# Nine period boundaries of a fused mixer move by one step

## The chip, the cores and the metric

The kernel runs on one core of a Trainium2 chip. The metric is the device time of one execution in microseconds; the time before is the median of three runs. A core has a matrix engine (TensorE; PE for its matmuls and PEld for its weight loads in the profile), VectorE (DVE), ScalarE (ACT), GpSimd (POOL) and SyncE (SP), which here issues the DMAs. Each engine runs its own instructions in the order in which the program lists them, and engines wait for each other by semaphores.

## The reference

Two parts follow each other. The first is a linear attention with a decaying state (batch B = 4, 8 heads, 768 tokens, 48 wide per head):

```
for t in range(S):
    cur = einsum('bhd,bhe->bhde', u * kt, vt)
    y[t] = einsum('bhd,bhde->bhe', rt, state + cur)
    state = w * state + einsum('bhd,bhe->bhde', kt, vt)
```

Its output, put together to x of 4 x 768 x 384, goes into a gated mixer:

```
h = relu(x @ w_in);  u, v = h[..., :512], h[..., 512:]
v_n = (v - mean(v)) / sqrt(var(v) + 1e-6)
v_s = einsum('ts,bsd->btd', w_spatial, v_n) + b_spatial
out = (u * v_s) @ w_out
```

## The kernel before, in words

**Attention.** The tokens of a batch are cut into 6 chunks of 128, so there are NM = 24 chunks, numbered through the batches; chunk m belongs to batch m // 6. For each chunk there are five pieces. `load_chunk` issues the two DMAs of a chunk (tiles rk and rkv, 512 and 648 KB). `prep` gives four parts that scale and combine the inputs on DVE and POOL and form the diagonal term (lines 279 to 308). `g1(m)` (lines 312 to 331) makes the scores and the state products with small matmuls into the PSUM tile ps: 32 in line 320 and 32 in line 329, or 16 there for the last chunk of a batch. `mid(m)` (339 to 360) masks the scores into the tile a (line 343, DVE), writes the state into the tiles sblk through `block` (lines 336 and 337, ACT) and updates the state on DVE. `g2(m)` (362 to 389) multiplies these with r and v, all in line 369: 48 matmuls with the state (24 for the first chunk of a batch) and 64 with a. `fin` casts the result to the pair xh and xl, a high and a low part (lines 399 and 404).

**Mixer.** The mixer works in steps, and each product is three matmuls of high and low parts (`mm3`, lines 427 to 430). A `moe_v` step makes the gate half of one chunk (9 matmuls, 512 columns), and after the third and sixth of a batch the normalisation follows on ACT and DVE. A `moe_u` step makes one 128-wide slice of the other half for 384 tokens (9 matmuls), `moe_sp` the spatial product for such a slice (18 matmuls, then an add on DVE, a product on POOL and a split into high and low on ACT and DVE), and `moe_out` the output product for 128 tokens (12 matmuls, a copy on ACT, an output DMA on SP). Every matmul has a weight load of its own. There are 28 steps a batch and 112 in all, in one list `steps` whose order is written out in lines 547 to 560.

**The order of the work.** The loop in lines 605 to 661 runs over periods i, one per chunk. At a period's start stand `g2(i)`, `fin(i)`, `g1(i + 1)` and `mid(i + 1)`, and the load of chunk i + 3. Then follow the mixer's steps from the list, until `done` has reached `n`, the number of steps that shall be done by the end of the period; between them, one ahead of each step, the four parts of the preparation of chunk i + 2. What remains of the parts follows after the last step. A step may hand work to a later step with `later`, which counts steps and not periods. Line 627 sets n: for the first six periods from the list FIRST, for the last all 112, and for the others an even deal:

```
int(10 + (i - 5) * 28 / 6)
```

which gives 14, 19, 24, 28, 33, 38, 42, ... 84, 89 for periods 6 to 22, that is 4 or 5 steps a period, and leaves 23 steps for period 23. TensorE's order is the order of the program: g2, g1, steps, g2, g1, steps.

## Time and profile before

| | before |
|---|---|
| median of 3 runs | 374.99 us (372.95 to 376.47) |
| profiled execution, its own time | 374.84 us |
| its span, first to last instruction | 373.1 us |
| TensorE matmuls busy | 340.5 us, 91% of the span |
| TensorE weight loads busy | 310.8 us, 83% |
| DVE, POOL, ACT busy | 200.5, 157.0, 148.0 us |
| mean granted TensorE clock | 0.993 of full speed |

How to read the rows: a row of the waits names who waited, for whom, the total in us, how often, and the longest. "issue" is time in which an engine waited for nothing that the profile shows. A row of the chain of waits has start, length and what ran. A row of the timeline has start, length, engine, line, operation, output and input, shape, and the number of instructions merged into it; an idle time in front of them stands in brackets. A row of the windows table has the stretch, its length, and for PE, PEld, DVE, ACT and POOL in turn the busy time with the number of instructions in brackets, then the granted clock, the DMA share and the rate in GB/s. Semaphore instructions are not in these counts. A row of the DMA queues has packets, MB and the time of the packets as a share of 16 engines' span. A row of the groups has line, engine, operation, tiles, shape and number, then busy time in all and mean ns of one, and the idle time before them. A row of the DMA issues has tiles, number, KB each and the us to landing.

### The profile page before, as it was taken

To read this page: it belongs to the slowest core of one execution; us is meant where nothing else is said; L and a number is where in the kernel's file an instruction comes from. 1 tells how busy PE (TensorE), PEld (TensorE's weight loads), DVE (VectorE), ACT (ScalarE), POOL (GpSimd) and SP (SyncE) were. 2 spreads that over 40 slices of the span, in tenths; PEclk is the share of its full clock that TensorE was granted. 3 is DMA by queue.
4 is the path that set the end of the run, shared out by engine and by line. 5 is a ranking of instruction groups with operands and counts; after the bars stand their busy time and mean duration, and the time that the engine had idled before them with its cause. 6 is when DMAs were issued, how large, how long until landed. Compare 5 with 4: busy or idle time off the path is not lost.

```text
span 373.1 us, 12304 instructions
## 1 busy us (share of the span) xinstructions
PE 340.5 (91%) x5479; PEld 310.8 (83%) x5479; DVE 200.5 (54%) x400; ACT 148.0 (40%) x325; POOL 157.0 (42%) x160
## 2 busy tenths in 40 slices
PE   2759669879999999899999989998999899999994
PEld 1427558779999998799999978898989898999994
DVE  7697855879645553664362625686451624433130
ACT  3154558584123234546131324645131336461211
POOL 5975555763554261645753444043652320013120
PEclk9999999999999999999999999999999999999998
DMA  7994755433031441333031352134041010000101
GB/s 251 413 372 135 267 204 176 170 129 105 29 124 70 131 154 52 117 132 129 2 129 65 129 186 67 72 129 131 0 152 45 2 66 4 0 0 2 56 9 63
DMA packets 14021, 41.69 MB, mean 112 GB/s; under 512 B 1680, under 2 KB 6416, under 8 KB 13968
## 3 DMA queue, kind: packets, MB, share of 16 engines
q1 hardware_dynamic: 13968, 40.90, 31.2%
q8 instruction: 43, 0.70, 0.8%
q14 instruction: 10, 0.08, 0.1%
HBM read 36.18 MB, written 4.72 MB: 110 GB/s over the span
## 4 chain that ended last, share of the span: by engine, by line
PE 82%; DVE 5%; ACT 4%; issue 4%; DMA 2%; POOL 2%; SPq 0%; ACTq 0%; DVEq 0%
PE pm L428 21%; PE pm L429 20%; PE pm L430 20%; PE xp L369 10%; PE ps L320 3%; PE ps L329 3%; DMA rkv<-rkvN 2%; ACT vs L472 1%; DVE a L343 1%; ACT ws_h L182 1%; DVE ws_l L183 1%; PE pm L498 1%; PE pm L503 1%; PE pm L499 1%; PE pm L226 1%
## 5 line engine op out<-in xcount | busy, mean ns | idle before, releaser
L516 POOL TENSOR_TENSOR g<-g,u 128x384 f32<-128x384 f32 x31 | 31.5, 1015 | 116.8 <-DVE g L515 116.7
L428 PE MATMUL pm<-ws_h,vnorm 128*128 128x384 f32 x192 | 64.9, 338 | 0.0
L430 PE MATMUL pm<-ws_h,vnorm 128*128 128x384 f32 x192 | 64.3, 335 | 0.0
L429 PE MATMUL pm<-ws_l,vnorm 128*128 128x384 f32 x192 | 64.2, 334 | 0.0
L303 POOL TENSOR_TENSOR a<-diag,dg 128x512 f32<-128x512 f32 x24 | 25.4, 1059 | 66.8 <-DVE dg L294 33.7
L182 ACT CAST gt<-g 128x384 fp32r<-128x384 f32 x32 | 16.4, 514 | 91.3 <-POOL g L516 89.3
L183 DVE TENSOR_TENSOR gt<-g,gt 128x384 fp32r<-128x384 f32 x32 | 20.9, 654 | 57.0 <-ACT gt L182 57.0
L428 PEld LDWEIGHTS pm<-ws_h,vnorm 128*128 128x128 f32 x192 | 36.0, 188 | 0.3
L429 PEld LDWEIGHTS pm<-ws_l,vnorm 128*128 128x128 f32 x192 | 36.0, 188 | 0.0
L430 PEld LDWEIGHTS pm<-ws_h,vnorm 128*128 128x128 f32 x192 | 36.0, 188 | 0.0
L428 PE MATMUL pm<-wo_h,gt 128*128 128x384 f32 x96 | 32.9, 343 | 0.0
L430 PE MATMUL pm<-wo_h,gt 128*128 128x384 f32 x96 | 32.3, 336 | 0.0
L429 PE MATMUL pm<-wo_l,gt 128*128 128x384 f32 x96 | 32.3, 336 | 0.0
L515 DVE TENSOR_TENSOR g<-pm,bb 128x384 f32<-128x384 f32 x32 | 17.7, 553 | 22.1 <-PE pm L430 22.0
L329 PE MATMUL ps<-rkv 64*64 64x48 f32 x704 | 17.8, 221 | 12.3 <-issue 8.7
L428 PE MATMUL pm<-wi_h,xh 128*128 128x512 f32 x72 | 28.7, 398 | 0.0
L430 PE MATMUL pm<-wi_h,xl 128*128 128x512 f32 x72 | 28.3, 393 | 0.1
L429 PE MATMUL pm<-wi_l,xh 128*128 128x512 f32 x72 | 28.3, 393 | 0.0
L369 PE MATMUL xp<-a,rkv 64*32 64x64 f32 x1536 | 24.1, 227 | 3.2 <-issue 3.2
L288 POOL TENSOR_TENSOR rkv<-rkv,ub 128x384 f32<-128x384 f32 x24 | 26.1, 1086 | 1.9
L449 DVE BATCH_NORM_STATS2 q<-vs 128x6 f32<-128x512 f32 x24 | 16.5, 687 | 18.6 <-ACT vs L442 18.6
L329 PEld LDWEIGHTS ps<-rkv 64*64 64x64 f32 x704 | 15.1, 139 | 13.5 <-issue 9.7
(112 smaller groups left out, 736.0 us busy)
## 6 DMA issues: line engine op xcount, KB each, us to landing
rkv<-rkvN SPq DMA_DIRECT2D x24, 648.0 KB, 5.8
rk<-rkT SPq DMA_DIRECT2D x24, 512.0 KB, 3.8
out<-ob SPq DMA_DIRECT2D x24, 192.0 KB, 1.9
raw<-w_in SPq DMA_DIRECT2D x6, 512.0 KB, 10.0
wst<-w_sp SPq DMA_DIRECT2D x12, 192.0 KB, 5.7
raw<-w_out SPq DMA_DIRECT2D x4, 384.0 KB, 8.1
bb<-b_sp SPq DMA_DIRECT2D x1, 384.0 KB, 5.6
ub<-uB SPq DMA_DIRECT2D x1, 192.0 KB, 6.6
```

Source lines behind the costliest of these rows:

```text
L182: nc.scalar.copy(hi, src)
L183: (eng or nc.vector).tensor_tensor(out=lo, in0=src, in1=hi.bitcast(F32), op=ALU.subtract)
L288: nc.gpsimd.tensor_tensor(out=rn, in0=rn, in1=ub, op=ALU.mult)
L303: nc.gpsimd.tensor_tensor(out=a.rearrange("s j p t -> s (j p) t"), in0=diag.unsqueeze(1).to_broadcast([P, H, HC]), in1=dg.rearrange("s j p ...
L329: nc.tensor.matmul(ps[64 * j:64 * j + 64, s0 // 64, 256 + p * D:256 + (p + 1) * D], t["kn"][s0:s0 + 64, h * D:h * D + 64], t["v"][s0:s0 + ...
L369: nc.tensor.matmul(xp[32 * g:32 * g + 32, z, jt * HC:(jt + 1) * HC], lhsT, rhs, start=(z, g) not in began, stop=True, skip_group_check=Tru ...
L428: nc.tensor.matmul(o, lh, rh, start=first, stop=False)
L429: nc.tensor.matmul(o, lh, rl, start=False, stop=False)
L430: nc.tensor.matmul(o, ll, rh, start=False, stop=last)
L449: nc.vector.bn_stats(out=q6[:, c % 3, :], in_=vs)
L515: nc.vector.tensor_tensor(out=g, in0=pm[:, 0:TH], in1=bb[:, ts_], op=ALU.add)
L516: (nc.vector if (b, t, d) == (B - 1, 1, ND - 1) else nc.gpsimd).tensor_tensor(out=g, in0=g, in1=u, op=ALU.mult)
```

## The change: nine numbers of done steps

A list of 24 numbers is added to the even deal of line 627. It is zero except in nine periods: the steps done by the end of periods 9, 13, 18 and 21 are one fewer, and by the end of periods 10, 15, 16, 19 and 20 one more. The order of the steps is the same, and so is everything that a step does; what differs is on which side of the next period's g2 and g1 nine of the steps stand.

| after period | done before | done after | step that changes sides |
|---|---|---|---|
| 9 | 28 | 27 | a moe_out of batch 0 goes behind |
| 10 | 33 | 34 | a moe_v of batch 1 comes ahead |
| 13 | 47 | 46 | a moe_sp of batch 1 goes behind |
| 15 | 56 | 57 | a moe_out of batch 1 comes ahead |
| 16 | 61 | 62 | a moe_v of batch 2 comes ahead |
| 18 | 70 | 69 | a moe_u of batch 2 goes behind |
| 19 | 75 | 76 | a moe_out of batch 2 comes ahead |
| 20 | 80 | 81 | a moe_sp of batch 2 comes ahead |
| 21 | 84 | 83 | a moe_out of batch 2 goes behind |

Periods 9 to 22 had 4, 5, 5, 4, 5, 5, 4, 5, 5, 4, 5, 5, 4 and 5 steps, and have 3, 7, 4, 4, 4, 6, 5, 5, 4, 3, 7, 5, 2 and 6.

```diff
+    ADJ = [0, 0, 0, 0, 0, 0, 0, 0, 0, -1, 1, 0, 0, -1, 0, 1, 1, 0, -1, 1, 1, -1, 0, 0]
...
-        n = 0 if i < 0 else FIRST[i] if i < NC else len(steps) if i == NM - 1 else int(10 + (i - 5) * 28 / 6)
+        n = 0 if i < 0 else FIRST[i] if i < NC else len(steps) if i == NM - 1 else int(10 + (i - 5) * 28 / 6) + ADJ[i]
```

## The prediction

> **What bounds the kernel now.** I read the page first, then the waits of TensorE alone, then the chain of waits, then the timeline around one stall, and last a table of windows that counts weight loads.

> ```profile
> span 373.1 us, 12304 instructions
> PE 340.5 (91%) x5479; PEld 310.8 (83%) x5479; DVE 200.5 (54%) x400; ACT 148.0 (40%) x325; POOL 157.0 (42%) x160
> q8 instruction: 43, 0.70, 0.8%
> PE ps L329 <- issue: 4.6, 5, 1.1
> ```

> The last line is the whole answer of the waits for TensorE from 88 us to the end. The first differing step falls in period 9, after 122 us, and the 23 steps of the last period are the same ones in the same order. So in the stretch that can change, the matrix engine waits for no other engine: it is idle 4.6 us in five places, always in line 329, on "issue". Removing all of it would be worth 4.6 us, 1.2% of the run; a reordering can win no more, since every step still costs the same TensorE time. It can lose more, by making PE wait for others.

> The five places in the chain of waits (start, length):

> ```profile
> 149.36 0.96 issue
> 218.50 0.95 issue
> 253.49 1.05 issue
> 273.35 0.62 issue
> 289.85 1.01 issue
> ```

> One of them in TensorE's timeline:

> ```profile
> 250.63 0.88 PE L369 MATMUL xp<-rk,sb 128*32 128x64 f32 x48
> 251.44 0.97 PE L369 MATMUL xp<-a,rkv 64*32 64x64 f32 x64
> 252.34 0.69 PE L320 MATMUL ps<-rk 64*64 64x64 f32 x32
> 252.85 0.63 PE L329 MATMUL ps<-rkv 64*64 64x48 f32 x30
> 254.54 0.31 PE L329 MATMUL ps<-rkv 64*64 64x48 f32 x2 [1.05 <-issue]
> ```

> I call lines 369, 320 and 329 between two periods' steps a burst, numbered by its g2: this is burst 19, 48+64+32+32 = 176 small matmuls with a weight load each (160 in bursts 10, 16 and 22, whose g1 is short, and 152 in 12 and 18, whose g2 is), and it stops before the last two. What is it waiting for? Counting loads answers. The windows below are (first row) burst 6 up to its stall, then bursts 11, 16, 19, 20 and 21 up to theirs, then one stall to the next, then from the stall of burst 11 to the starts of bursts 13 and 14, then the whole of burst 22, and last 6 us of steps. The count behind PEld is what to read.

> ```profile
> 76.85:79.90 3.05, 2.59 (x151) 2.22 (x151) 1.22 (x3) 2.99 (x7) 2.56 (x2) 1.00 0.37 115
> 146.72:149.90 3.18, 2.64 (x159) 2.32 (x159) 0.14 (x1) 2.94 (x5) 1.36 (x2) 1.00 0.36 109
> 215.75:219.00 3.25, 2.75 (x155) 2.43 (x155) 0.56 (x1) 1.55 (x4) 2.79 (x3) 1.00 0.21 68
> 250.62:254.20 3.58, 2.87 (x175) 2.55 (x174) 1.85 (x3) 3.52 (x7) 0.35 (x1) 1.00 0.44 135
> 270.60:273.60 3.00, 2.75 (x164) 2.44 (x163) 1.03 (x2) 0.51 (x1) 1.25 (x3) 1.00 0.36 101
> 287.04:290.40 3.36, 2.81 (x170) 2.49 (x169) 1.23 (x3) 1.19 (x4) 1.00 (x1) 1.00 0.03 7
> 254.20:273.60 19.40, 18.81 (x255) 18.20 (x255) 9.99 (x17) 4.54 (x12) 9.83 (x11) 1.00 0.18 54
> 273.60:290.40 16.80, 15.89 (x254) 15.28 (x254) 6.81 (x13) 5.34 (x14) 6.26 (x7) 1.00 0.26 91
> 150.20:169.25 19.05, 18.93 (x251) 16.99 (x250) 12.22 (x27) 9.96 (x21) 10.19 (x10) 1.00 0.31 103
> 150.20:187.85 37.65, 37.53 (x517) 35.10 (x516) 20.14 (x41) 15.85 (x34) 21.47 (x21) 1.00 0.26 85
> 300.65:303.40 2.75, 2.75 (x161) 2.53 (x160) 0.36 (x1) 1.33 (x4) 0.00 (x0) 1.00 0.25 83
> 244.40:250.40 6.00, 6.00 (x36) 5.98 (x35) 5.42 (x12) 3.02 (x8) 1.94 (x2) 1.00 0.41 158
> ```

> **Which block ends stall.** Let the position be the number of loads from the burst's start to the block end. Stalls: 151 (burst 6), 155, 159, 163, 169, 174. None: in burst 13 a block ends at 255 - 250 = 5 and the next at 132; in burst 14 at 4 x 127.3 - 516 = -7 and 120. Burst 6's stall shows that 151 stalls:

> ```profile
> 80.27 0.26 PE L329 MATMUL ps<-rkv 64*64 64x48 f32 x2 [0.83 <-issue]
> ```

> Between 132 and 151 I need the moment at which a fetch starts. The transfer rate in 40 slices of 167.0 to 169.3 us (before burst 13), of 216.5 to 218.5 (inside burst 16), and the pause at a burst's start:

> ```profile
> GB/s 0 0 0 0 0 0 0 0 285 0 0 0 0 0 0 0 0 0 0 0 0 0 0 0 0 0 0 0 0 0 0 0 0 0 0 0 0 0 0 0
> GB/s 0 0 0 0 0 0 0 0 0 328 0 0 0 0 0 215 369 338 399 215 430 399 369 215 399 246 62 31 0 31 0 0 31 0 0 0 0 31 0 31
> 300.69 0.72 PEld L369 LDWEIGHTS xp<-rk,sb 128*32 128x32 f32 x48 [0.25 <-issue]
> ```

> The lone 16 KB packet comes at 167.5, 1.8 us before burst 13 (previous block end at 5), and at 217.0, 1.2 us into burst 16 (previous end at 155 - 127 = 28). If the fetch is asked for when execution is T loads ahead of the previous end, the 3.0 us between the two are 0.017(28 - T) + 0.25 + 0.171(T - 5), so T is 20. This is an estimate from two packets; 0.4 us more or less between them would move T to 23 or 17. It gives a rule: with the previous end at 20 or more loads into the burst, the full stall (0.95 to 1.05 us, once 0.62); for each load less, 0.154 us off, and 0.25 at once for the pause. Likewise 0.154 off for each load that the position lies past the burst's 176.

> **The change, part by part.** Work is only moved across bursts. By the loops a moe_sp step has 18 pairs (6 tiles by 3), moe_out 12 (4 by 3), moe_v and moe_u 9 (3 by 3). A step moved ahead of a burst lowers all positions in it by its pairs; one moved behind raises them.

> - Burst 11 (moe_v ahead): 159 to 150, previous end at 23: stalls, 0.96 stays. Bounds 0.5 (T = 24 for this one) and 1.05.
> - Burst 16 (moe_out ahead): 155 to 143, previous end at 16, four loads before T: 0.95 - 0.25 - 0.62 leaves 0.1. Bounds 0 and 0.95.
> - Burst 19 (moe_u behind): 174 to 183, 7 past the end: 1.05 - 1.08, nothing left; I leave 0.1. Bounds 0 and 1.05.
> - Burst 20 (moe_out ahead): 163 to 151, where burst 6 stalls: 0.62 stays or becomes the usual 0.95; I add 0.2.
> - Burst 21 (moe_sp ahead): 169 to 151: 1.01 stays.
> - Burst 14 (moe_sp behind): 120 to 138, previous end at 11, nine loads before T: 1.6 us off, no stall. Bounds 0 (as at 132) and +0.95 (as at 151).
> - Bursts 10, 17, 22 (moe_out behind, moe_v ahead, moe_out behind): counted from the stall nearest, with 160 + 48, 160 + 48 and 176 + 51 loads from burst to burst, 159 + 208 - 255 = 112 becomes 124, 155 + 127 - 208 = 74 becomes 65, 169 + 127 - 227 = 69 becomes 81. All below 132; the ends 127 later lie 16 or more past the burst, which takes 2.5 us off: 0.

> What the moved steps issue elsewhere goes with them: the relu and statistics of moe_v, the relu of moe_u, the copy and output DMA of moe_out, the add, product and split of moe_sp.

> ```profile
> L516 POOL TENSOR_TENSOR g<-g,u 128x384 f32<-128x384 f32 x31 | 31.5, 1015 | 116.8 <-DVE g L515 116.7
> out<-ob SPq DMA_DIRECT2D x24, 192.0 KB, 1.9
> rkv<-rkvN SPq DMA_DIRECT2D x24, 648.0 KB, 5.8
> ```

> The four parts of a chunk's preparation are issued one a step from the period's start, so where a period begins a step earlier or later they change sides on POOL with one 1.0 us product of moe_sp at most; the chunk is read a period later, and POOL idles 117 us in front of such products: 0, or 1 us if that slack were gone. On SP, two output issues pass ahead of the loads of chunks 19 and 23, and two fall behind those of 13 and 25 (there is no 25). A load waits for g2 in any case, lands in 5.8 us and is prepared in the next period; an output falling behind one lands later, and its buffer is asked for again only by the second next moe_out: 0, or the 1.9 us of one output on ACT, in front of nothing that PE reads before five steps have passed. Two short periods have to cover the state chain from burst to burst:

> ```profile
> 248.79 0.35 ACT L337 COPY sb<-t 64x192 f32<-64x192 f32 x1
> 291.25 0.75 DVE L343 COPY_PREDICATED a<-mask,ps 128x512 f32<-128x512 uint32 x1 [0.49 <-PE ps L329]
> 292.64 0.35 ACT L337 COPY sb<-t 64x192 f32<-64x192 f32 x1
> ```

> Period 21 keeps two steps, at least 21 x 0.171 = 3.6 us. Its state copy ended at 292.99, 1.7 us after the mask copy that starts right behind burst 21: hidden. Period 18 keeps three moe_u steps; burst 19 began at 250.63 and would begin 9 x 0.171 = 1.54 earlier, at 249.09, while the copy ends at 249.14. The first 24 of the 48 loads use the older state, 0.4 us of cover, so I cost it at 0; without that cover each us of delay costs one. The loads of a later chunk go out behind g2 as before.

> Sum: 374.84 (the profiled execution: span 373.1 and 1.7 around it) - 0.85 - 0.95 + 0.2 = 373.2. Against the median of 374.99 that is 373.4.

> [...]

> **Rivals.**
> *No net gain.* With T at 11 the stall of burst 16 stays and burst 14 gains one: 374.84 - 0.95 + 0.95 + 0.2 = 375.0; with T at 16 only the first, 374.1. A few more semaphore instructions in front of these bursts would do the same. For it: no row between 132 and 151. Against it: both packet times. Chance 0.30.
> *All stalls go.* [...] Chance 0.08. [...]
> *Slower: period 18 starves burst 19.* The third norm's low half and moe_v's statistics now stand before the state update of chunk 18 on DVE:

> ```profile
> 240.19 0.68 DVE L479 TENSOR_TENSOR vnorm<-vs,vnorm 128x512 fp32r<-128x512 f32 x1
> 240.79 0.69 DVE L449 BATCH_NORM_STATS2 q<-vs 128x6 f32<-128x512 f32 x1
> 254.29 1.15 DVE L479 TENSOR_TENSOR vnorm<-vs,vnorm 128x512 fp32r<-128x512 f32 x1 [0.58 <-ACT vnorm L474]
> ```

> If this isn't made up behind it, the copy comes 1.4 us later, 1.9 if L479 runs at its slow 1.15: minus 0.4 of cover, PE waits 1.5, the lead is spent and burst 19 keeps its 1.05: 374.84 - 0.85 + 1.5 + 0.2 = 375.7. It decides from 0.4 us of lateness on. Against it: the same work leaves the queue behind the update, so the chain should end when it did. Chance 0.15.

> **Numbers.** Forecast 0.47, between 372.4 (both stalls gone whole, and 0.5 from burst 11) and 374.2 (burst 19 keeps its 1.05). The runs of before reach from 372.95 to 376.47, so a median of a few runs moves by a microsecond. The range 371.3 to 375.9 leaves out the case without stalls and large waits. One per cent (3.75 us), about what a measurement of this kernel can tell from no change, needs four of five stalls gone: faster 0.09. Slower by as much needs a wait of over 5 us that no row shows: 0.06. Within: 0.85.

> **What would show it.** Right: the same wait list with three entries near 3 us, in bursts 11, 20 and 21, and nothing in 14, 16 and 19; burst 19 starting when the state copy ends. Wrong: a wait of L369 for ACT or DVE; an "issue" stall in burst 14 or 16 (T too large); none in 11, 20, 21 (T too small).

## The result, and the profile after

| | before | after |
|---|---|---|
| median, 20 runs each | 375.45 us (372.95 to 379.79) | 373.41 us (371.03 to 375.79) |
| ratio | | 0.9946, 95% interval 0.9922 to 0.9969 |
| profiled execution, span | 374.84, 373.1 us | 371.81, 370.1 us |

The change makes the kernel 0.54% faster, 2.0 us of 375. The forecast was 1.6 us and 373.4.

The changed kernel has two lines more near its top, so line 320 is now 322, 329 is 331 and 369 is 371. First the waits of TensorE from 88 us to the end, and then the places on the chain of waits (start, length):

```profile
PE ps L331 <- issue: 3.1, 3, 1.2
```

```profile
150.59 1.18 issue
271.99 1.15 issue
289.90 0.81 issue
```

It is still the only wait, three times instead of five, 3.1 us instead of 4.6. The load counts tell which bursts these are, and what became of the others. The rows are bursts 11, 16, 19, 20, 21 and 14 from their start, the ones with a stall cut inside it; then three long stretches: the start to burst 7, burst 7 to burst 23, and the rest.

```profile
148.03:150.90 2.87, 2.56 (x150) 2.20 (x150) 0.00 (x0) 2.81 (x6) 2.33 (x3) 1.00 0.28 70
217.22:219.90 2.68, 2.68 (x159) 2.45 (x160) 0.28 (x1) 1.26 (x4) 0.86 (x1) 1.00 0.45 119
247.16:249.90 2.74, 2.74 (x177) 2.50 (x176) 1.55 (x2) 2.65 (x5) 0.00 (x0) 1.00 0.19 46
269.43:272.50 3.07, 2.56 (x152) 2.20 (x152) 1.33 (x3) 1.76 (x5) 2.75 (x3) 1.00 0.03 8
287.34:290.30 2.96, 2.56 (x153) 2.20 (x152) 1.07 (x2) 1.06 (x3) 2.02 (x3) 1.00 0.02 6
184.16:186.90 2.74, 2.74 (x177) 2.51 (x176) 1.01 (x2) 0.51 (x1) 2.01 (x2) 1.00 0.26 60
0.00:87.14 87.14, 65.48 (x1405) 51.46 (x1405) 65.18 (x129) 46.37 (x105) 55.55 (x62) 0.98 0.64 227
87.14:309.96 222.82, 219.68 (x3666) 205.77 (x3665) 117.76 (x234) 81.53 (x184) 96.50 (x91) 1.00 0.27 93
309.96:370.10 60.14, 55.30 (x410) 53.58 (x409) 18.00 (x38) 20.27 (x38) 7.15 (x7) 0.99 0.06 21
```

The stalls stand at loads 150, 152 and 152 of bursts 11, 20 and 21 (forecast 150, 151, 151). Bursts 16, 19 and 14 run through, 160, 176 and 176 loads in one piece. The three long stretches of the kernel before, cut at the same instructions:

```profile
0.00:87.90 87.90, 64.65 (x1405) 50.80 (x1405) 64.72 (x129) 46.26 (x105) 55.41 (x62) 0.98 0.63 225
87.90:313.05 225.15, 220.56 (x3666) 206.43 (x3665) 117.78 (x235) 81.48 (x183) 94.44 (x91) 1.00 0.27 92
313.05:373.10 60.05, 55.26 (x410) 53.58 (x409) 17.98 (x38) 20.28 (x38) 7.16 (x7) 0.98 0.06 21
```

Between burst 7 and burst 23 the profiled execution gained 2.3 us: 1.5 by idle time that went, 0.9 by the same 3666 matmuls being busy for less. The 0.8 us at the start lie ahead of the first step that changes sides, so the change didn't make them; the tail is the same. So the two profiles differ by 3.0 us, the medians by 2.0.

### The profile page after: what moved, and what is told of

The parts are those of the page before. It is cut to its first block, busy times and chain, and to the rows that moved or that the text cites. A ratio compares the mean times of both kernels' runs of the same rounds, so it can differ in the third digit from the quotient of the medians.

```text
span 370.1 us, 12305 instructions
## 1 busy us (share of the span) xinstructions
PE 340.5 (92%) x5479; PEld 310.8 (84%) x5479; DVE 200.9 (54%) x400; ACT 148.2 (40%) x325; POOL 159.2 (43%) x160
## 4 chain that ended last, share of the span: by engine, by line
PE 84%; ACT 4%; DMA 3%; DVE 3%; issue 3%; SPq 1%; POOL 1%; ACTq 0%; DVEq 0%
PE pm L430 22%; PE pm L431 21%; PE pm L432 21%; PE xp L371 10%; PE ps L322 3%; PE ps L331 3%; DMA rkv<-rkvN 2%; DMA wst<-w_sp 1%; PE pm L228 1%; ACT vs L474 1%; SPq L92 1%; ACT vnorm L476 1%; DVE ws_l L185 1%; PE pm L500 1%; PE pm L505 1%
## 5 line engine op out<-in xcount | busy, mean ns | idle before, releaser
L518 POOL TENSOR_TENSOR g<-g,u 128x384 f32<-128x384 f32 x31 | 31.5, 1017 | 115.8 <-DVE g L517 115.8
L293 POOL TENSOR_TENSOR rkv<-rkv,tn 128x384 f32<-128x384 f32 x24 | 26.7, 1114 | 0.0
L289 POOL TENSOR_TENSOR rkv<-rkv 128x384 f32<-128x384 f32 x24 | 25.5, 1062 | 2.3 <-DMA rkv<-rkvN 2.3
## 6 DMA issues: line engine op xcount, KB each, us to landing
rkv<-rkvN SPq DMA_DIRECT2D x24, 648.0 KB, 5.9
out<-ob SPq DMA_DIRECT2D x24, 192.0 KB, 1.9
wst<-w_sp SPq DMA_DIRECT2D x12, 192.0 KB, 6.2
ub<-uB SPq DMA_DIRECT2D x1, 192.0 KB, 6.6
```

The source lines that it names most:

```text
L289: (nc.vector if DV0 and m == 0 else nc.gpsimd).tensor_tensor(out=rn, in0=rn, in1=kn, op=ALU.mult)
L293: (nc.vector if DV0 and m == 0 else nc.gpsimd).tensor_tensor(out=kn, in0=kn, in1=tn_f, op=ALU.mult)
L518: (nc.vector if (b, t, d) == (B - 1, 1, ND - 1) else nc.gpsimd).tensor_tensor(out=g, in0=g, in1=u, op=ALU.mult)
```

## The experiments

Each kernel is built from the changed one; only the list of differences, or the filler pairs described, are edited. Ratios are to the kernel before, run on the same chip in the same session.

**Two moves alone.**

```diff
-    ADJ = [0, 0, 0, 0, 0, 0, 0, 0, 0, -1, 1, 0, 0, -1, 0, 1, 1, 0, -1, 1, 1, -1, 0, 0]
+    ADJ = [0, 0, 0, 0, 0, 0, 0, 0, 0, 0, 0, 0, 0, 0, 0, 1, 0, 0, -1, 0, 0, 0, 0, 0]
```

> Only the two moves that the theory credits: the moe_out step ahead of burst 16 and the moe_u step behind burst 19; the other seven boundaries are as before. Theory (the stalls are block ends of the instruction stream that fall late in a burst): stalls stay in bursts 11, 20 and 21, none in 16 and 19; TensorE waits about 2.6 to 3.1 us in three places from 88 us on; 1.5 to 2.0 us faster than the kernel before, that is as fast as the whole change. Rival (the gain comes from all nine boundaries, that is from the lengths of the periods): two ninths of the gain, under 0.6 us, and no tie between position and stall.

Measured: 0.9957 (0.9927 to 0.9987), 1.6 us faster. Its waits of TensorE from 88 us on:

```profile
PE ps L331 <- issue: 2.9, 3, 1.1
```

Two of nine moves give most of the gain, and within the intervals all of it. The stalls are again those of bursts 11, 20 and 21, whose positions these two moves leave as they were.

**The seven others alone.**

```diff
-    ADJ = [0, 0, 0, 0, 0, 0, 0, 0, 0, -1, 1, 0, 0, -1, 0, 1, 1, 0, -1, 1, 1, -1, 0, 0]
+    ADJ = [0, 0, 0, 0, 0, 0, 0, 0, 0, -1, 1, 0, 0, -1, 0, 0, 1, 0, 0, 1, 1, -1, 0, 0]
```

> The seven other moves, without the two. Theory: five stalls in bursts 11, 16, 19, 20 and 21 at positions 150, 155, 174, 151 and 151, together 4.6 to 5.1 us; the time of the kernel before within 0.5 us. Rival (lengths of the periods): most of the change's 2 us is kept.

Measured: 1.0004 (0.9973 to 1.0035), and five stalls:

```profile
PE ps L331 <- issue: 4.5, 5, 1.2
```

So the lengths of the periods as such are worth nothing that can be told from noise (0.3% either way).

**A phase shift without any moved step.** The list of differences is all zero, and one moe_out step of period 9 begins with 32 small load-and-matmul pairs (16 calls of two).

```diff
+    PADS = {26: 16}
...
+    def fillers(pm):
+        for _ in range(pad[0]):
+            nc.tensor.matmul(pm[0:32, 0:64], eye[:, 0:32], eye[:, 0:64], start=True, stop=True,
+                             skip_group_check=True, tile_position=(0, 0))
...
+        fillers(pm)
...
```

> No step changes sides: the kernel before, with 32 small load-and-matmul pairs (the burst's own shape, into a tile that is overwritten right after; their results are not used) in the third step of period 9, ahead of burst 10. Every block end from there on lies 32 loads earlier in its burst. Theory: previous block ends become 0 (burst 11), -5 (16), 15 (19), 4 (20), 10 (21): none of these stalls; burst 17 goes from 74 to 42 and must stall in full at position 170, burst 22 from 70 to 38 (position 165, 5 past its 160: about 0.2); burst 12 ends 9 past its 152: none. TensorE waits 0.9 to 1.3 us in all instead of 4.6; the pairs cost 0.5 us; 2.5 to 3.3 us faster than before (ratio 0.992). Rival (moved steps or period lengths matter): stalls stay where they were, 0.5 us slower.

Measured: 0.9932 (0.9901 to 0.9963), 2.6 us faster although the kernel does more. The waits of TensorE, the fillers and burst 17 in its timeline:

```profile
PE ps L332 <- issue: 1.0, 1, 1.0
```

```profile
131.81 1.97 PE L440 MATMUL pm<-eye 128*32 128x64 f32 x32
...
230.56 0.88 PE L372 MATMUL xp<-rk,sb 128*32 128x64 f32 x48
231.37 0.97 PE L372 MATMUL xp<-a,rkv 64*32 64x64 f32 x64
232.27 0.69 PE L323 MATMUL ps<-rk 64*64 64x64 f32 x32
232.79 0.57 PE L332 MATMUL ps<-rkv 64*64 64x48 f32 x25
234.39 0.33 PE L332 MATMUL ps<-rkv 64*64 64x48 f32 x7 [1.02 <-issue]
```

All five stalls are gone and one has come, in burst 17, which had none before: 48 + 64 + 32 + 25 = 169 matmuls in, where 170 was forecast. It is the number of instructions ahead of a burst that decides, not which steps they belong to. Only the fillers cost more than the 0.5 us that I gave them, 2.0.

The instruction queue's own packets say the same. In the twelve profiles of this document there are 39 places where the weight loads stand still on "issue" inside a burst, from burst 6 on. With the semaphore instructions, which the views leave out, the number of TensorE's instructions ahead of each of them leaves 193 or 194 when it is divided by 256; and at each, TensorE went on 1.2 to 1.6 us after the last 16 KB packet of the instruction queue had landed.

**A deal worked out from the rule.**

```diff
-    ADJ = [0, 0, 0, 0, 0, 0, 0, 0, 0, -1, 1, 0, 0, -1, 0, 1, 1, 0, -1, 1, 1, -1, 0, 0]
+    ADJ = [0, 0, 0, 0, 0, 0, 0, 0, 0, 0, 2, 0, 0, 0, 0, 1, 0, 0, -1, 2, -1, 0, 0, 0]
```

> A deal worked out from the rule: the steps done are two more after period 10 (18 loads ahead of burst 11, previous block end at 14), one more after 15, one fewer after 18, two more after 19 (24 ahead of burst 20, previous end at 12) and one fewer after 20 (18 behind burst 21, position 187, 11 past the burst). Theory: no stall from 88 us on but for remainders of 0.1 us, 4 to 4.6 us faster than the kernel before (ratio 0.988). Rival (the order of steps in the short period 20, two steps long, makes burst 21 wait for the state copy): a wait of line 371 in burst 21 and under 3 us gained. If fetches are asked for earlier or later than 20 loads ahead, bursts 11 and 16 (previous end at 14 and 15) show it first.

Measured: 0.9889 (0.9838 to 0.994), 4.2 us faster. Every "issue" stall of the matmuls is gone, but in its place there is one wait, not the one that the rival named:

```profile
PE pm L430 <- ACT gt L184: 1.3, 1, 1.3
```

In period 21 a moe_out step asked for the split of the last moe_sp product, with one moe_v step between them. That slice's add on DVE ended at 293.72, but its product on POOL (the last row) stood behind the preparation of chunk 23:

```profile
293.17 0.55 DVE L517 TENSOR_TENSOR g<-pm,bb 128x384 f32<-128x384 f32 x1
```

```profile
290.84 1.01 POOL L518 TENSOR_TENSOR g<-g,u 128x384 f32<-128x384 f32 x1 [3.83 <-DVE g L517]
291.82 1.02 POOL L289 TENSOR_TENSOR rkv<-rkv 128x384 f32<-128x384 f32 x1
292.91 1.22 POOL L290 TENSOR_TENSOR rkv<-rkv,ub 128x384 f32<-128x384 f32 x1
294.09 1.01 POOL L293 TENSOR_TENSOR rkv<-rkv,tn 128x384 f32<-128x384 f32 x1
295.06 0.99 POOL L518 TENSOR_TENSOR g<-g,u 128x384 f32<-128x384 f32 x1
```

**The same, mended.** Burst 21 now stands between that moe_v step and the moe_out step, and covers the chain.

```diff
-    ADJ = [0, 0, 0, 0, 0, 0, 0, 0, 0, 0, 2, 0, 0, 0, 0, 1, 0, 0, -1, 2, -1, 0, 0, 0]
+    ADJ = [0, 0, 0, 0, 0, 0, 0, 0, 0, 0, 2, 0, 0, 0, 0, 1, 0, 0, -1, 2, 2, 0, 0, 0]
```

> The deal without stalls, mended where its profile showed a wait of 1.3 us of moe_out for its split input: burst 21 now stands behind the moe_v step (two steps more by the end of period 20 instead of one fewer; 27 loads ahead of it, previous block end at 15.5), so that it covers that chain. Theory: no wait of TensorE from 88 us on but for remainders of 0.1 us; 4.4 to 4.8 us faster than before (ratio 0.9875). Rival (the short period 21, two steps, starves burst 22; or T is 16 and burst 21 keeps a part): a wait of line 371 or a stall in burst 21, no faster than the deal before it.

Measured: 369.59 us against 375.22, ratio 0.9858 (0.9827 to 0.9889), 5.3 us faster than before, where 4.4 to 4.8 were expected, and clear of the change as well. The wait list from 88 us on is empty. From burst 7 to burst 23 TensorE is busy all the time, with the same 3666 matmuls in 219.03 us instead of 225.15:

```profile
90.51:309.54 219.03, 219.03 (x3666) 205.53 (x3665) 115.60 (x234) 81.39 (x182) 95.53 (x91) 1.00 0.28 94
```

**Period 18 with two steps.**

```diff
-    ADJ = [0, 0, 0, 0, 0, 0, 0, 0, 0, 0, 0, 0, 0, 0, 0, 1, 0, 0, -1, 0, 0, 0, 0, 0]
+    ADJ = [0, 0, 0, 0, 0, 0, 0, 0, 0, 0, 0, 0, 0, 0, 0, 1, 0, 0, -2, 0, 0, 0, 0, 0]
```

> As the kernel with two moves, but two moe_u steps go behind burst 19, so that period 18 has two steps. Theory: the state copy comes 1.2 us too late for burst 19 (it ended at 249.1 where the burst would begin at 247.55, with 0.4 of cover), TensorE waits 0.8 to 1.3 us in line 371 or before it; burst 19's block end lies at 192, no stall. So 0.8 to 1.3 us slower than the kernel with two moves, 0.5 to 1 faster than before. Rival (the state copy comes earlier when TensorE does, or enough older work covers it): no wait, as fast as the kernel with two moves.

Measured: 0.9974 (0.9938 to 1.001), 0.6 us slower than two moves alone by the two ratios, whose intervals overlap. A wait came, but of 1.5 us where 0.8 to 1.3 was expected, and in another place:

```profile
PE ps L331 <- issue: 2.6, 3, 1.2
PE pm L432 <- DVE vnorm L481: 1.5, 1, 1.5
```

Burst 19 began at 249.44, while the second half of the state copy ran from 249.35 to 249.70: it waited next to nothing (its first load came 0.25 us after the step's last, the same pause as in the kernel before at 250.63), since its first 24 loads read the older state. What was late is the low part of the last norm, which two steps later the first moe_sp reads. With one step fewer ahead of the burst it is issued behind it, and so behind the state update and the scaling of the next chunk on DVE:

```profile
257.40 1.23 DVE L286 TENSOR_TENSOR rk<-rk,tt 128x1024 f32<-128x1024 f32 x1
258.55 1.48 DVE L481 TENSOR_TENSOR vnorm<-vs,vnorm 128x512 fp32r<-128x512 f32 x1
257.50 1.98 POOL L293 TENSOR_TENSOR rkv<-rkv,tn 128x384 f32<-128x384 f32 x1
```

Elsewhere in this trace the scaling (L286) took 1.22 us with POOL idle, the subtraction (L481) 0.69 and POOL's product 1.0. Here they ended one after the other, the scaling at 258.63, the product at 259.48 and the subtraction at 260.03: the product took 1.98 and the subtraction 1.48, 0.98 and 0.79 longer than elsewhere. Whether the two engines held each other up, and how, was not tried.

**Fillers in the changed kernel: 4, 8, 2 and 4 pairs again.** The list of differences is the change's; the second step of period 10 begins with 1, 2 or 4 calls of the filler above. This lowers the position in bursts 11, 20, 21 and 19 by 2, 4 or 8 loads, to find the edge.

> The changed kernel with 4 such pairs in the second step of period 10: previous block ends fall by 4 loads, to 18.5 (burst 11), 19.5 (20 and 21), 52 (19, position 179, 3 past the end). Theory with T = 20: half to two thirds of each stall is left: about 0.45, 0.6 and 0.6 us, and 0.5 in burst 19; 2.2 us in all. If T is 16 or less, the three stay whole (0.8 to 1.2 each); if it is 24, they are gone. Rival (a stall needs only the position within the burst, whatever the step pace before it): whole stalls.

> As before, with 8 pairs: previous block ends at 14.5 (burst 11), 15.5 (20 and 21), 48 (19, position 175). Theory with T = 20: 0 to 0.1 us in bursts 11, 20 and 21, and a whole stall of 0.95 to 1.05 us in burst 19 again; about 1 us in all. If T is 16, about 0.5 each in 20 and 21.

> The changed kernel with 2 of the small pairs in the second step of period 10. The 4 pairs left a stall of 0.74 us in burst 21 and none in bursts 11 and 20, so the edge of the previous block end lies between 20 and 22 loads, not at 20 with a slow fall below it. Edge at 21 to 22: burst 11 (20.5) has none or a small one, bursts 20 (22) and 21 (23.5) whole ones of 0.6 to 1.2 us, burst 19 (5 past the end) at most 0.3; about 2 us in all. Rival (the fetch itself takes longer or shorter by 0.3 us from one to the next, and no edge can be told): all three between 0.3 and 0.9.

> The kernel with 4 pairs a second time, unchanged. Edge at 21 to 22: again a stall in burst 21 (0.5 to 1 us), again none in 11 and 20, 0.3 to 0.6 in 19. Rival (fetch times vary): other bursts among 11, 20 and 21 stall than the first time.

Each was run once, so their times (371.80, 372.83, 377.83 and 372.70 us, in the order above) prove nothing; what counts are the traces. The idle time of the weight loads at the block end, us (in brackets the loads from the burst's start to it; where nothing stalls, worked out from the neighbours). The loads show short stalls that the matmul rows hide:

| fillers | burst 11 | burst 20 | burst 21 | burst 19 |
|---|---|---|---|---|
| 0 (the change) | 1.31 (150) | 1.28 (152) | 0.93 (152) | 0 (184) |
| 2 | 0.21 (148) | 1.12 (150) | 1.58 (151) | 0.32 (182) |
| 4 | 0 (146) | 0.21 (148) | 0.86 (149) | 0.81 (180) |
| 4 again | 0 (146) | 0.34 (148) | 1.03 (149) | 0.68 (180) |
| 8 | 0 (142) | 0 (144) | 0 (145) | 1.50 (176) |

Burst 11 with 2 fillers, and bursts 20 and 21 of the second run with 4:

```profile
155.35 0.55 PEld L332 LDWEIGHTS ps<-rkv 64*64 64x64 f32 x28 [0.21 <-issue]
```

```profile
273.69 0.55 PEld L332 LDWEIGHTS ps<-rkv 64*64 64x64 f32 x28 [0.34 <-issue]
291.46 0.54 PEld L332 LDWEIGHTS ps<-rkv 64*64 64x64 f32 x27 [1.03 <-issue]
```

Up to 146 loads there is no stall, at 148 one of 0.2 to 0.3 us, from 149 to 152 a whole one of 0.9 to 1.6 us. The packets of the instruction queue show what changes. The transfer rate in 40 slices of 0.05 us, from 270.5 us (burst 20 begins at 270.96) and from 287.6 us (burst 21 begins at 288.04), in the second run with 4:

```profile
GB/s 0 0 0 0 0 0 0 0 0 0 0 328 0 0 0 0 0 0 0 0 0 0 0 0 0 0 0 0 0 0 0 0 0 0 0 0 0 0 0 0
GB/s 0 0 0 0 0 0 0 0 0 0 0 0 0 0 0 0 0 0 0 0 0 0 0 0 0 0 0 0 0 0 0 0 328 0 0 0 0 0 0 0
```

The packet starts 0.1 us into burst 20, whose block ends at 148, but 1.2 us into burst 21, whose block ends at 149. With 8 fillers (144 and 145) the packets start 0.65 and 0.38 us before these bursts, and nothing stalls. Why the one load from 148 to 149 makes about a microsecond stays open. At the other end the stall fades beyond the burst's last load, as forecast. Two of the rivals on record fall: T at 16 (no stall is left at 142 to 145), and the position alone without the pace ahead of it, by which 146 would stall like 150. Of the last two expectations the edge held, and the rival of varying fetch times fell: the same bursts stalled in both runs with 4 fillers, within 0.2 us.

## Why the prediction was right

It was right in the mechanism: which stalls go, which stay, and at which load. It was right in the time as well (373.4 forecast, 373.41 measured), but the agreement to 0.1 us is luck: runs lie 5 us apart, the forecast started from a median of 374.99 where 20 runs gave 375.45, and two of its terms were too small and partly made up for each other.

- *What bounds it*: TensorE alone, idle in five places. The mended deal confirmed it from the other side: with every wait gone from 88 us on, 5.3 us were won (4.2 to 6.5). But the prediction called 4.6 us, the idle time of the matmuls, the most that a reordering can win, and a stall costs more than that entry. What it costs shows from the first weight load of a burst to the first of the step behind it. This is burst 19, with its stall in the kernel before and without it in the changed one:

```profile
250.63 0.71 PEld L369 LDWEIGHTS xp<-rk,sb 128*32 128x32 f32 x48 [0.25 <-ACT vs L472]
254.54 0.19 PEld L329 LDWEIGHTS ps<-rkv 64*64 64x64 f32 x2 [1.17 <-issue]
254.78 0.19 PEld L428 LDWEIGHTS pm<-ws_h,vnorm 128*128 128x128 f32 x1
```

```profile
247.21 0.72 PEld L371 LDWEIGHTS xp<-rk,sb 128*32 128x32 f32 x48 [0.25 <-ACT sb L339]
250.00 0.19 PEld L430 LDWEIGHTS pm<-xh,wi_h 128*128 128x128 f32 x1
```

  That is 4.15 us against 2.79. In the kernel before, the nine other bursts with a full g2 from 7 to 22 take 2.79 each, and the five with a stall 4.01, 3.99, 4.15, 3.73 and 4.07: 6.0 us too much, not 4.6. The mended deal takes 6.1 us less over the stretch from burst 7 to burst 23.
- *Burst 16 and burst 19*: 0.85 and 0.95 gained, forecast. No stall is left in either, and by the length of the burst they gained 1.20 and 1.36. The two moves alone measured 1.6 us.
- *Bursts 11, 20 and 21*: staying, as forecast, at the forecast loads. The matmuls' idle time is 3.1 us instead of the forecast 2.8 in all; by the length of the bursts they cost 0.45 us more than before (3.9 against 3.4), where 0.2 was forecast. With these sizes the sum is 2.1 us instead of 1.6, and the medians differ by 2.0.
- *Burst 14, and bursts 10, 17 and 22*: nothing, as forecast. The seven moves together measured nothing beyond noise.
- *Short periods*: 0, as forecast. In the change the state copy that burst 19 needs ended at 246.92 and the burst began at 247.21. The slower rival didn't come. With two steps in period 18, one fewer than in the change, TensorE did wait 1.5 us, but for the norm's low part and not for the state copy.
- *T = 20 loads ahead*: a little too small, and the fall below the edge too slow. With T = 20 the stall should be whole at 148 and half of it left at 146; it was 0.2 to 0.3 us at 148 and gone at 146. The two packet times gave 20, with 17 to 23 as bounds; the fillers give 148 - 127 = 21. No term of the sum hung on the difference.
- *Block ends outside the stalls*: of the 17 bursts from 88 us on in the kernel before 12 ran without a stall, and no block end within steps cost anything (from 88 us on the weight loads waited on "issue" 5.2 us at the five stalls, 3.0 us at the starts of 11 bursts, and nowhere in the steps between). Where a whole block fell into a burst, its end cost up to 1.46 us of idle matmuls (burst 21 with 2 fillers).

## What to carry to other kernels

An idle matrix engine with "issue" as the releaser, in the middle of many small matmuls, is worth counting: if the instructions from one such place to the next are always a multiple of one number (here 256), and a packet of the instruction queue lands shortly before TensorE goes on (here 1.2 to 1.6 us), the instruction stream arrives too late. What helped here was to keep a whole block (256 instructions, some 127 load-and-matmul pairs and a semaphore instruction or two) from falling into one run of small instructions, by moving long work across it (5.3 us in the mended deal) or by shifting the phase (2.6 us). Every step that then changes sides must be followed to its consumer two steps on: here the same kind of move that won a microsecond brought waits of 1.3 and 1.5 where a split or a norm was asked for earlier than DVE, ACT and POOL could give it.

## What the runs showed of the hardware that was not expected

The 32 filler pairs took 1.97 us, some 60 ns a pair, while line 372's 48 pairs of the same shape (128 x 32 weights, 64 columns; line 369 in the kernel before) took 0.88, 18 a pair. The fillers all stand at `tile_position=(0, 0)` and write the same output again and again; line 372 goes round four column positions, 0, 32, 64 and 96. Which of the two is the cause was not tried.

The spread between runs of one kernel goes with the granted clock. Of the changed kernel's 20 runs, the five with a mean granted clock up to 0.985 took 375.0 us on average, the nine with 0.990 or more 372.7. Where it is lost can be seen in profiles only. These are the first 88 us of the kernel before and of the kernel with 2 fillers, which is the same program up to there; its profiled execution took 377.83 us in spite of fewer stalls, and had got 26 matmuls less far by then (the number before the DMA share is the clock).

```profile
0.00:88.00 88.00, 64.75 (x1412) 50.90 (x1416) 64.82 (x129) 46.36 (x105) 55.41 (x62) 0.98 0.63 224
```

```profile
0.00:88.00 88.00, 65.57 (x1386) 51.37 (x1387) 61.54 (x123) 45.38 (x102) 54.85 (x62) 0.92 0.64 224
```
